# Spreading inverse row sums over the partitions: two half precision products in place of one fp32 product

## The chip, the cores and the metric

The kernel runs on one core of one Trainium2 chip. The core's engines are TensorE (PE in the profile, with its weight loads as PEld), VectorE (DVE), ScalarE (ACT), GpSimd (POOL) and SyncE (SP), which here only issues DMAs. The metric is the device time of one execution in microseconds; the time of a kernel is the median of several executions.

## What is computed

The reference is a clustered attention followed by a maxout feed-forward layer, on 4 batches, 8 heads, 768 positions and 64 features a head. Queries and keys are assigned to the nearest of 16 centroids of their head; a query sees only keys of its own cluster.

```python
q_assign = np.argmax(np.einsum('bhsd,hcd->bhsc', q_n, c_n), axis=-1)
k_assign = np.argmax(np.einsum('bhsd,hcd->bhsc', k_n, c_n), axis=-1)
mask = q_assign[:, :, :, None] == k_assign[:, :, None, :]
scores = scale * np.matmul(q, k.transpose(0, 1, 3, 2))
scores = np.where(mask, scores, -1000000000.0)
scores = scores - np.max(scores, axis=-1, keepdims=True)
attn = np.exp(scores)
attn = attn / (np.sum(attn, axis=-1, keepdims=True) + 1e-09)
x = np.matmul(attn, v)          # heads side by side: 3072 tokens of 512
h = np.maximum(np.maximum(x @ w1, x @ w2), x @ w3)
out = h @ w_out
```

What matters here is the division by the row sum. The kernel leaves the exponentials undivided, multiplies them with `v`, and multiplies the outcome with the inverse of the row sum afterwards.

## The kernel before

**Visits and steps.** The kernel works in 32 visits: for each batch, four pairs of heads times two halves of the query positions (`gi`, 384 positions each). A visit has six steps, one for each of its two heads and three tiles of 128 queries. A step (`scores`, lines 500 to 518) makes the scores of 128 queries against 768 keys with four products on PE (two at line 505, two at line 507), has DVE scale them and find the row's extreme value (510), ACT take the exponential and leave the row's sum in `rs` (513), ACT copy the outcome to half precision (515), and POOL or DVE, in turn, subtract that copy from the fp32 value (517), so that two half precision numbers stand for one of higher precision. The odd steps, the last of every visit among them, use POOL. A DMA then transposes both halves into `pt` (518).

**After a visit** come three more pieces. `av_sums` (524 to 532) takes the visit's row sums `rs`, 128 queries on the partitions and six numbers in each (three tiles, two heads). ACT adds 1e-9 (526), DVE inverts (527), and PE spreads them: for each tile and head one product with the inverse sums as weights, one column repeated 64 times, and the identity as the moving operand, puts the inverse sum of query n into column n on all 64 partitions of that head (532). It is an fp32 product; in the trace each of the six leaves two records, so a group is 12 records. `av` (534 to 546) makes the attention's output with 36 products of 64 weight columns and 384 moving columns (540). The two heads' products go to the lower and upper half of the array's columns, and so do those of line 532. `x_split` (548 to 559) copies the spread inverse sums from PSUM to SBUF on ACT (551), multiplies them with the output on DVE (553 or 555), and splits the result into two half precision numbers on POOL (557, 558).

**The rest** is preparation and the feed-forward layer. For each batch and pair of heads, `prep_units` loads queries and keys, scales and splits them, and finds the clusters (products at 444 and 448 of 64 weight columns, then DVE and POOL at 455 to 486, with DMAs that move halves between partitions). `v_prep` does likewise for `v`. The feed-forward layer's hidden products (585: 128 weight columns, 384 moving ones, twelve to a unit) and output products (619: 128 weight columns, 512 moving ones, 18 to a unit) run among the score steps of the next half batch. The very last feed-forward units stand alone at the end, from 807 us on.

**What sets the order.** Each piece of work gets a priority from the step in which it is planned (`spread`, `put`, `paced`, `plan`). A scheduler with a timing model of its own then sets the order of instructions on each engine from the priorities and from what it thinks is ready. The engines take that order as it stands. `av_sums` and `x_split` of a visit get a priority one step after the place where they are planned, and `av` five steps before it; all three are planned in the second step of the next visit. PSUM has three large buffers (`big`): one holds the output and the spread sums of a visit from the first product of `av_sums` until `x_split` has read it, and the others serve the scores.

## Time and profile before

| what | value |
|---|---|
| median of 3 runs | 858.13 us (857.68 to 858.15) |
| the profiled execution: its own time | 856.58 us |
| its span, from the first to the last instruction | 854.8 us |
| mean granted clock of TensorE | 0.928 |
| products at line 532 | 384 records, 34.6 us busy |
| ACT step at line 526, x32 | 216 ns each |
| DVE step at line 527, x32 | 182 ns each |

The profile is of one execution. A time "busy" is the time in which an engine had something running; products on PE are pipelined, so the length of a record includes the tail that runs beside the next one, and the pace of PE is read from the start of one record to the start of the next. The chain of waits is followed back from the last instruction to what released it, step by step; its shares say which engine held the end up. "Idle before" is the time that an engine stood still ahead of an instruction, with what ended it. A line such as `L532` is the kernel's line; a shape such as `128*64` is rows and columns of the array.

### The profile page before, as it was taken

What the parts mean: (1) busy time and instruction counts of PE and PEld (TensorE: products, weight loads), DVE (VectorE), ACT (ScalarE), POOL (GpSimd) and SP (SyncE); (2) the same over time, 40 slices, a digit from 0 to 9 for tenths busy, and PEclk for the clock granted to TensorE, in tenths of its full rate; (3) what the DMA queues carried; (4) which work ended last, traced back from release to release, by engine and by line L of the source; (5) the groups of instructions that cost most, each with busy time, mean ns of one, the idle gap of its engine ahead of it and who ended that gap; (6) DMA issues with size and microseconds to landing.
All of it is one profiled execution on the core that took longest, in us unless ns stands there. A gap on an engine that the chain in (4) does not pass through costs nothing.

```text
span 854.8 us, 13244 instructions
## 1 busy us (share of the span) xinstructions
PE 708.7 (83%) x4629; PEld 390.5 (46%) x4629; DVE 556.0 (65%) x1150; ACT 474.2 (55%) x837; POOL 456.1 (53%) x448
## 2 busy tenths in 40 slices
PE   2254452667989999998987899999798999999997
PEld 1122121333555455554544455555345555555563
DVE  6967858879588486368675685569768764665020
ACT  5657555776754546564663566665457465566201
POOL 1267467498676544255873654366666643454221
PEclk9995665797999999999989999999899999999999
DMA  6698795899588766678977966688978976667300
GB/s 235 127 218 178 182 222 113 185 228 201 125 178 168 154 118 127 138 140 164 188 150 155 190 133 125 146 166 159 194 158 162 154 138 136 124 112 119 86 1 37
DMA packets 329154, 128.90 MB, mean 151 GB/s; under 512 B 304384, under 2 KB 315520, under 8 KB 329088
## 3 DMA queue, kind: packets, MB, share of 16 engines
q1 hardware_dynamic: 329088, 128.06, 72.4%
q8 instruction: 36, 0.59, 0.3%
q14 instruction: 30, 0.25, 0.1%
HBM read 31.49 MB, written 6.29 MB: 44 GB/s over the span
## 4 chain that ended last, share of the span: by engine, by line
PE 52%; DVE 16%; DMA 10%; POOL 9%; issue 7%; ACT 4%; SPq 1%; POOLq 0%; DVEq 0%; ACTq 0%
PE one L585 22%; PE one L619 10%; PE big L540 8%; DMA stage<-in_qk_dram 5%; PE big L505 4%; PE big L507 4%; DVE big L510 4%; PE big L532 2%; POOL hl L517 2%; DMA stage<-in_v_dram 2%; DMA wd<-in_moe_w_dram 2%; POOL qk L417 2%; DVE hl L517 2%; DVE wf L196 2%; DMA pt<-hl 1%
## 5 line engine op out<-in xcount | busy, mean ns | idle before, releaser
L517 POOL TENSOR_TENSOR hl<-e,hl 128x768 f16<-128x768 f32 x96 | 158.6, 1652 | 162.3 <-ACT hl L515 162.3
L510 DVE TENSOR_SCALAR_CACHE_REDUCE big<-big,nsc 128x768 f32<-128x768 f32 x192 | 193.8, 1019 | 63.3 <-PE big L507 61.7
L585 PE MATMUL one<-x,w16a 128*128 128x384 f16 x1152 | 207.7, 328 | 7.0 <-DVE vpow L109 3.2
L505 PE MATMUL big<-qk 128*128 128x512 f16 (+1 forms) x384 | 105.3, 358 | 65.8 <-ACT e L513 27.5
L513 ACT ACTIVATE big<-big,nm 128x768 f32<-128x768 f32 x96 | 83.9, 874 | 127.5 <-DVE big L510 103.3
L585 PEld LDWEIGHTS <-w16a 128*128 128x128 f16 x1152 | 110.8, 98 | 87.7 <-issue 18.0
L513 ACT ACTIVATE e<-big,nm 128x768 f32<-128x768 f32 x96 | 86.7, 903 | 74.7 <-DVE big L510 65.1
L540 PE MATMUL big<-pt,v 128*64 128x384 f16 x1152 | 118.6, 344 | 1.0 <-DMA pt<-hl 0.9
L507 PE MATMUL big<-qk 96*128 96x512 f16 (+1 forms) x384 | 107.0, 359 | 13.2 <-DMA qk<-cl_t 12.1
L517 DVE TENSOR_TENSOR hl<-big,hl 128x768 f16<-128x768 f32 x96 | 91.2, 950 | 33.7 <-ACT hl L515 33.7
L585 PE MATMUL one<-x,w16b 128*128 128x384 f16 x576 | 102.8, 329 | 0.0
L505 PEld LDWEIGHTS <-qk 128*128 128x128 f16 x384 | 36.0, 102 | 123.9 <-issue 91.6
L540 PEld LDWEIGHTS <-v 128*64 128x64 f16 x1152 | 72.8, 116 | 36.8 <-issue 10.1
L515 ACT CAST hl<-e 128x768 f16<-128x768 f32 x96 | 80.1, 835 | 1.6
L515 ACT CAST hl<-big 128x768 f16<-128x768 f32 x96 | 76.7, 799 | 1.8
L585 PEld LDWEIGHTS <-w16b 128*128 128x128 f16 x576 | 55.8, 98 | 39.8 <-issue 4.4
L557 POOL TENSOR_SCALAR x<-xs 128x384 f16<-128x384 f32 x32 | 16.8, 524 | 90.7 <-DVE xs L553 78.1
L507 PEld LDWEIGHTS <-qk 96*128 96x128 f16 x384 | 40.7, 106 | 46.3 <-DMA qk<-cl_t 12.0
L381 DVE TENSOR_REDUCE q_m<-stage 128x1 f32<-128x768 f32 x32 | 30.1, 948 | 40.9 <-DMA stage<-in_qk_dram 40.9
L619 PE MATMUL one<-wo,wf_h 128*128 128x512 f16 x216 | 50.9, 379 | 0.8 <-ACT o L628 0.8
L597 DVE SCALAR_TENSOR_TENSOR wf_h<-one,wf_h 128x384 f32<-128x384 f32 x48 | 26.4, 551 | 38.6 <-PE one L585 34.6
L417 POOL TENSOR_TENSOR qk<-stage,qk 128x768 f16<-128x768 f32 x30 | 49.4, 1656 | 0.9 <-ACT qk L416 0.8
(142 smaller groups left out, 927.8 us busy)
## 6 DMA issues: line engine op xcount, KB each, us to landing
stage<-in_qk_dram SPq DMA_DIRECT2D x32, 384.0 KB, 4.2
wd<-in_moe_w_dram SPq DMA_DIRECT2D x18, 512.0 KB, 4.9
out_dram<-o SPq DMA_DIRECT2D x24, 256.0 KB, 2.8
qk<-qk SPq DMA_DIRECT2D x15, 384.0 KB, 4.7
qk<-qk SPq DMA_DIRECT2D x30, 192.0 KB, 3.8
stage<-in_v_dram SPq DMA_DIRECT2D x12, 384.0 KB, 4.9
pt<-hl SPq DMA_TRANSPOSE x192, 4.0
wd<-in_moe_w_out_dram SPq DMA_DIRECT2D x6, 512.0 KB, 4.5
```

The costliest lines, as they stand in the source:

```text
L381: nc.vector.tensor_reduce(m2[:, i : i + 1], x, axis=AX.X, op=ALU.max, apply_absolute_value=True)
L417: last["lo"] = nc.gpsimd.tensor_tensor(t[:, AQ, i], x, t[:, BQ, i], op=ALU.subtract)
L505: nc.tensor.matmul(t[:, lo:hi], aq[:, qs], ak[:, lo:hi], start=True, stop=False)
L507: last["pe"] = nc.tensor.matmul(t[:, lo:hi], bq[0:K2, qs], bk[0:K2, lo:hi], start=False, stop=True)
L510: last["nm"] = nc.vector.tensor_scalar(e, e, nsc[b, h // 2], 3.0e38, op0=ALU.mult, op1=ALU.min, accum_out=nm)
L513: last["exp"] = nc.scalar.activation(x, e, AF.Exp, bias=nm, scale=-1.0, accum_out=r)
L515: nc.scalar.copy(hl[:, 0, :], x)
L517: eng.tensor_tensor(hl[:, 1, :], x, hl[:, 0, :], op=ALU.subtract)
L540: nc.tensor.matmul(t[D * i : D * i + D, 0:NB], v[:, i, kt, a], pts[i][:, :, c * QT + kt, :], start=(n == 0), stop=(n == len(parts) - 1),)
L585: nc.tensor.matmul(t[:, 0:NB], w16[jt // JA][:, jt % JA, wa, i, ct], x16[b, gi, ct][:, xa, :], start=(n == 0), stop=(n == 3 * CT - 1),)
L597: nc.vector.scalar_tensor_tensor(m, t[:, 0:NB], 2.0**-24, ms[jt], op0=ALU.mult, op1=ALU.max)
L619: nc.tensor.matmul(t[:, 0:DM], h16[jt][:, ha, tt * P : (tt + 1) * P], wo16[0][:, jt, wa, :], start=(n == 0), stop=(n == 3 * JT - 1),)
```

## The change

The inverse sums are made into a pair of half precision numbers. After the reciprocal, ACT scales them by 2^14 and rounds to half precision (the first of the pair), and DVE scales the fp32 value by the same factor and subtracts the first (the second of the pair). In place of one fp32 product, PE makes two half precision products for each tile and head, which add up in PSUM: six become twelve. A half precision copy of the identity is the moving operand; POOL makes it once at the start. The copy from PSUM in `x_split` takes the factor out again.

```diff
+RSC = 2.0**14
...
+    identh = cpool.tile([P, P], F16, name="identh")
+    nc.gpsimd.tensor_copy(identh, ident)
...
         nc.scalar.activation(rs, rs, AF.Copy, bias=1.0e-9)
         nc.vector.reciprocal(rs, rs)
+        r16 = sb.tile([P, 2, G, 2], F16, tag="r16", name="r16", bufs=2)
+        nc.scalar.activation(r16[:, 0], rs, AF.Copy, scale=RSC)
+        nc.vector.scalar_tensor_tensor(r16[:, 1], rs, RSC, r16[:, 0], op0=ALU.mult, op1=ALU.subtract)
         for g in range(G):
             at = 512 + g * P
-            for i in range(2):
-                w = rs[:, g, i : i + 1].broadcast_to([P, D])
-                nc.tensor.matmul(t[D * i : D * i + D, at : at + P], w, ident, start=True, stop=True)
+            for a in range(2):
+                for i in range(2):
+                    w = r16[:, a, g, i : i + 1].broadcast_to([P, D])
+                    o = t[D * i : D * i + D, at : at + P]
+                    nc.tensor.matmul(o, w, identh, start=(a == 0), stop=(a == 1))
...
-        nc.scalar.copy(xs, t[:, 512 : 512 + NB])
+        nc.scalar.activation(xs, t[:, 512 : 512 + NB], AF.Copy, scale=1.0 / RSC)
```

The scheduler sets the order anew on every engine. The lines of the changed kernel stand 3 lower up to `av_sums` (505 becomes 508, 527 becomes 530) and 8 lower behind it (585 becomes 593, 619 becomes 627, `av` at 540 becomes 548); the spreading products, 532 before, are at line 540 then. Over the whole program, the order before goes between products of 64 weight columns and products of 128 on PE 204 times, the order after 270 times.

On PE, the eleventh visit's spreading products (325 us in the profile before), between hidden products of the feed-forward layer; `x` and `w16b` are that layer's operands, `v` and `pt` those of `av`. Before:

```order
L585 LDWEIGHTS w16b
L585 MATMUL one<-x_2177,w16b 128x384
L532 MATMUL big<-ident,rs 64x128 x6
L540 LDWEIGHTS v_2019
L540 MATMUL big<-pt,v_2019 64x384
L585 LDWEIGHTS w16b
L585 MATMUL one<-x_734,w16b 128x384
```

After, in the same visit, with `r` the new half precision pair and `qk` the operands of the scores:

```order
L593 MATMUL one<-x_2251,w16b 128x384
L540 LDWEIGHTS r_3052
L540 MATMUL big<-identh,r_3052 64x128
L508 LDWEIGHTS qk
L508 MATMUL big<-qk 128x512
L508 LDWEIGHTS qk
L508 MATMUL big<-qk 128x256
L510 LDWEIGHTS qk
L510 MATMUL big<-qk 128x512
L510 LDWEIGHTS qk
L510 MATMUL big<-qk 128x256
L540 LDWEIGHTS r_3052
```

The six products stood together, with the first `av` product behind them; now one of the twelve stands alone ahead of a step's score products, a second one alone ahead of the next step's, and the others follow in two pieces.

On PE, the 28th visit's (718 us before), among the output products of the feed-forward layer (`wo`, `wf_h`). Before:

```order
L619 MATMUL one<-wo_586,wf_h 128x512
L532 MATMUL big<-ident,rs 64x128
L619 LDWEIGHTS wf_h
L619 MATMUL one<-wo_586,wf_h 128x512
L532 MATMUL big<-ident,rs 64x128
L540 LDWEIGHTS v_6336
```

After:

```order
L627 MATMUL one<-wo_597,wf_h 128x512
L540 LDWEIGHTS r_7417
L540 MATMUL big<-identh,r_7417 64x128
L627 LDWEIGHTS wf_h
L627 MATMUL one<-wo_597,wf_h 128x512
L540 LDWEIGHTS r_7417
L540 MATMUL big<-identh,r_7417 64x128
```

Here three of the six stood alone between output products; now ten of the twelve do.

On DVE, the 16th visit's inverse sums (437 us before), at a change of batch; `sc_s` and `vpow` are scales of `v`, `hl` the split exponentials, `vf_h` the hidden layer. Before:

```order
L527 RECIPROCAL rs<-rs 128x6
L111 TENSOR_SCALAR sc_s<-sc_s 128x1
L517 TENSOR_TENSOR hl<-big,hl 128x768
L597 SCALAR_TENSOR_TENSOR vf_h<-one,vf_h 128x384
L510 TENSOR_SCALAR big,nm<-big,nsc 128x768
```

After, with the added step at line 533:

```order
L530 RECIPROCAL rs<-rs 128x6
L113 RECIPROCAL sc_s<-vpow 128x1
L114 TENSOR_SCALAR sc_s<-sc_s 128x1
L520 TENSOR_TENSOR hl<-big,hl 128x768
L533 SCALAR_TENSOR_TENSOR r_4356<-rs,r_4356 128x6
L605 SCALAR_TENSOR_TENSOR vf_h<-one,vf_h 128x384
```

The added step stands a subtraction behind the reciprocal, and the maximum of the hidden layer stands behind it; it waits for ACT's half of the pair, which stands behind an exponential on ACT.

## The prediction

> **What bounds the kernel now.** I read the head of the page and its chain of waits first, to see which engine sets the end, then a table by stretches, because an average over the span hides where that is so.
>
> ```profile
> span 854.8 us, 13244 instructions
> PE 708.7 (83%) x4629; PEld 390.5 (46%) x4629; DVE 556.0 (65%) x1150; ACT 474.2 (55%) x837; POOL 456.1 (53%) x448
> ...
> PE 52%; DVE 16%; DMA 10%; POOL 9%; issue 7%; ACT 4%; SPq 1%; POOLq 0%; DVEq 0%; ACTq 0%
> ```
>
> TensorE (PE) holds 52% of the chain that ended last, VectorE (DVE) 16%, ScalarE (ACT) 4%. The windows say where (length, busy time and instruction count of PE, PE's weight loads, DVE, ACT and POOL, then the granted clock and the DMA load):
>
> ```profile
> 0.00:250.00 250.00, 136.67 (x796) 68.20 (x796) 190.47 (x419) 159.77 (x268) 149.59 (x161) 0.80 0.81 183
> 250.00:400.00 150.00, 148.80 (x1001) 83.83 (x1002) 98.30 (x194) 80.03 (x144) 80.95 (x75) 1.00 0.73 147
> 400.00:500.00 100.00, 84.42 (x547) 46.89 (x545) 67.54 (x154) 52.79 (x97) 60.03 (x55) 0.93 0.80 164
> 500.00:600.00 100.00, 98.32 (x686) 55.91 (x685) 68.69 (x133) 62.29 (x112) 53.13 (x50) 1.00 0.74 144
> 600.00:660.00 60.00, 50.86 (x338) 27.29 (x338) 44.61 (x102) 33.33 (x62) 38.06 (x34) 0.94 0.86 175
> 660.00:807.00 147.00, 146.47 (x1029) 84.39 (x1026) 79.73 (x139) 81.45 (x151) 65.80 (x64) 1.00 0.70 129
> ```
>
> In three stretches (250 to 400, 500 to 600, 660 to 807) PE is busy for 393.6 of 397 us: there every tenth of a microsecond of PE counts, and nothing else does. In the other three (0 to 250, 400 to 500, 600 to 660) PE stands idle for 138 of 410 us, waiting for the preparation of the next pair or batch, and there DVE, ACT, POOL and DMA set the pace. The same query kept to line 532 says how many of the 32 groups of the changed product fall in each; a group is 12 records, two for each of six products:
>
> ```profile
> 250.00:400.00 150.00, 6.96 (x72) 4.31 (x72) 1.00 0.73 147
> 500.00:600.00 100.00, 4.14 (x48) 2.70 (x48) 1.00 0.74 144
> 660.00:807.00 147.00, 7.62 (x84) 4.97 (x84) 1.00 0.70 129
> ```
>
> So 17 groups (204 records) lie where PE is full, and 15 where it isn't.
>
> **The products themselves.** The timeline of PE in a full stretch (start, time with the pipeline's tail, what, count; the pace is read from start to start):
>
> ```profile
> 754.28 2.11 PE L585 MATMUL one<-x,w16a 128*128 128x384 f16 x12
> 756.32 0.88 PE L532 MATMUL big<-ident,rs 128*64 128x128 f32 x12
> 757.02 0.33 PE L540 MATMUL big<-pt,v 128*64 128x384 f16 x1
> 757.28 1.80 PE L585 MATMUL one<-x,w16a 128*128 128x384 f16 x10
> 758.92 0.49 PE L505 MATMUL big<-qk 128*128 128x512 f16 x2
> ```
>
> A group of six fp32 products takes 0.70 us (756.32 to 757.02). Its two heads go to the two halves of the array's columns and run side by side, so it is three slots of 0.23 us. No row shows a half precision product of 128 columns on half the array. The nearest are those of 256 columns at lines 444 and 448:
>
> ```profile
> 386.26 0.28 PE L444 MATMUL big<-qk,cw 128*64 128x256 f16 x2
> 386.37 0.28 PE L448 MATMUL big<-qk,cw 128*64 128x256 f16 x2
> ```
>
> A pair of those takes 0.11 us. If the time goes with the columns, a pair of 128 takes 0.055 us; if weight loads limit it, up to 0.11. I take 0.06, since pairs of 384 and of 256 columns both follow their columns here. The added work on PE is then six slots of 0.06, 0.36 us a group in place of 0.70.
>
> **How the order cuts the groups up.** The saving would be 17 times 0.34, or 5.8 us, if the twelve products stood together. The order shows that they don't. In the full stretches the old order has 58 slots of fp32 products (51, and 7 because of lone products); the new one has 121 slots, not 102. That is 58 x 0.23 - 121 x 0.06 = 13.3 - 7.3 = 6.0 us saved. The `av` products at line 540, 36 in a group, are cut less often: 312 slots for 320, and at 0.163 us each (10 products of line 585, also of 384 columns, take 1.64 us) that saves 1.3 us more. Against this stand the changes between half-array and full-array products, of which the new order has 146 there, where the old has 104. What one costs is read above: the lone `L540` takes 0.26 us until the next full product starts, 0.10 more than its 0.163; twelve products of line 585 take 2.04 us ahead of line 532, 0.07 more than twelve times 0.164. Lone products in the middle of line 619 show it again:
>
> ```profile
> 717.96 0.43 PE L532 MATMUL big<-ident,rs 128*64 128x128 f32 x2
> 718.33 0.39 PE L619 MATMUL one<-wo,wf_h 128*128 128x512 f16 x1
> 718.65 0.43 PE L532 MATMUL big<-ident,rs 128*64 128x128 f32 x2
> 719.01 0.39 PE L619 MATMUL one<-wo,wf_h 128*128 128x512 f16 x1
> ```
>
> I take 0.10 us a change; 42 more are +4.2 us. PE in the full stretches: -6.0 - 1.3 + 4.2 = **-3.1 us**, all of it on the path. In the other stretches PE's saving is hidden behind what it waits for: 0, at best -2.
>
> **The added ACT and DVE steps.** Their nearest rows are the steps on the same tile and a DVE step with two tensors from SBUF, like the added one:
>
> ```profile
> L526 ACT ACTIVATE rs<-rs 128x6 f32<-128x6 f32 x32 | 6.9, 216 | 0.0
> L527 DVE RECIPROCAL rs<-rs 128x6 f32<-128x6 f32 x32 | 5.8, 182 | 8.1 <-ACT rs L526 8.1
> L399 DVE SCALAR_TENSOR_TENSOR nsc<-q_p 128x1 f32<-128x1 f32 x16 | 6.6, 414 | 0.0
> L399 DVE SCALAR_TENSOR_TENSOR nsc<-q_p x16: 133/140/1557, 8.5 to 656.7; 128x1 f32<-128x1 f32 x16
> ```
>
> The ACT step costs 0.216 us. The DVE step costs 0.14 us if it runs freely and up to 1.56 if it is held; I take line 399's mean, 0.41. In the full stretches PE's queue covers both. In the others they count in part: DVE's 16% of the chain is 137 us, and if all of it lies outside the full stretches, where DVE is busy for 303 us, 0.45 of its time there is on the path; for ACT the same gives 34 of 246 us, or 0.14. For 15 groups that is 15 x 0.41 x 0.45 + 15 x 0.216 x 0.14 = 2.8 + 0.4 = **+3.2 us**. What is queued behind the new waits: on DVE, behind the step that waits for ACT's half, the next score reduction (line 510) and the maximum of the hidden layer (line 597); on ACT, behind the copy that waits for the reciprocal, the next exponential; on PE, which takes its queue in order, the next head's score products.
>
> The other edits cost nothing that shows. The scaled copy in place of the plain one (line 551) goes from 479 ns to what line 595 takes for the same shape, 490, on an engine that is 55% busy:
>
> ```profile
> L551 ACT COPY xs<-big 128x384 f32<-128x384 f32 x32 | 15.3, 479 | 44.1 <-PE big L540 44.0
> L595 ACT ACTIVATE wf_h<-one 128x384 f32<-128x384 f32 x24 | 11.8, 490 | 43.2 <-PE one L585 30.8 <-DVE wf_h L597 7.7 <-DVE cl_m L462 3.2
> ```
>
> If that cover goes, it is 32 x 0.011 = 0.35 us. POOL's one cast of the identity stands at the start, ahead of its first work. The queue of DMAs holds the same 394 transfers, some of them moved among each other. I can't price that move; two batch boundaries with the same work show what order can do there: between 400 and 500 PE idles 15.6 us, between 600 and 660 9.1, so I allow 3 us either way for it in the range and nothing in the sum.
>
> **Sum.** -3.1 + 3.2 = +0.1 us against the profiled execution's 856.58 us (span 854.8 and 1.8 around it), so 856.7. That execution lies 1.55 us under the median of 858.13, so a median of about 858.2: no change. About 0.2% (1.7 us) is what a measurement of this kernel can tell from none.
>
> **The rivals.** *Slower: the DVE step is held by POOL and the groups wait for it.* At line 399 one step of 128x1 took 1.56 us, just as long as a POOL subtraction beside it ran:
>
> ```profile
> 287.32 1.56 DVE L399 SCALAR_TENSOR_TENSOR nsc<-q_p 128x1 f32<-128x1 f32 x1
> ...
> 287.22 1.64 POOL L517 TENSOR_TENSOR hl<-e,hl 128x768 f16<-128x768 f32 x1 [5.70 <-ACT hl L515]
> ```
>
> The last head step of every visit is one whose subtraction is POOL's, and the sums are ready as it starts, so the added step may meet it nearly every time. With 1.0 us each, 15 x 1.0 x 0.45 = 6.8 in place of 2.8, and PE waits as well where it had no slack; it already did here:
>
> ```profile
> 471.88 0.88 PE L532 MATMUL big<-ident,rs 128*64 128x128 f32 x12 [0.48 <-DVE rs L527]
> ```
>
> With half a microsecond at a third of the 17 groups, +2.8: 858.2 + 4.0 + 2.8 = 865. It decides from a mean of about 0.7 us for the step. The Trainium skill, SBUF — State Buffer, Who interferes with whom, says that a DVE instruction with two SBUF inputs and a GpSimd instruction that reads SBUF exclude each other for the whole instruction; by that rule, with which line 399 agrees (1.56 us beside 1.64), the step is held whenever POOL is busy.
>
> *No gain on PE: a half precision pair costs 0.11 us, not 0.06.* Its weight load would be the limit. Then 121 slots cost 13.3 us, PE gains nothing but loses 2.9 to the changes, and the time is 858.2 + 6.0 = 864. The pairs of 256 columns can't speak against it, as 0.11 is what they take anyway. The Trainium skill, TensorE: Matmul & The Clock Gate, Back-to-back issue gap, gives about 81 ns a product for a stream of loads and products of 128 columns, 56 without the loads; with 81 a slot the sum would be 2.5 us higher, an estimate from that page. No run here shows such a pair yet.
>
> *Faster: the extra changes fall where PE waits anyway, or cost less.* PE's saving then stays near 7.3 us in the full stretches, and DVE's step runs freely (0.14 us, 15 x 0.14 x 0.45 = 0.9): 858.2 - 4.2 - 1.9 = 852. For it: the order was made with products split wherever PE had room. Against: in the full stretches PE has 3.4 us of room in all.
>
> **How the numbers follow.** My forecast, that both sides cancel within some 3 us, has 0.46, of which 0.11 falls below 856.4, 0.25 within 0.2%, 0.10 above 859.8. The held DVE step has 0.24, no gain on PE 0.05, the faster rival 0.25. So faster 0.36, same 0.25, slower 0.39. The range goes from the faster rival less the 3 us for order at a boundary (849) to the held step plus 3 (868); the forecast's own range is 855 to 861.
>
> **What would show it.** In the profile after: groups of half precision products of about 0.36 us where they stand together; 0.10 us at each change; PE's busy time down by some 3 to 5 us; the added DVE line with a mean near 0.4 us, and with lengths that end with POOL's; the idle time of PE ahead of the products still under 8 us. The forecast is wrong if the full stretches shrink by over 6 us, if they don't shrink at all, or if the stretches at the batch boundaries change by more than 4 us.

## The result and the profile after

| | before | after |
|---|---|---|
| median of 5 runs | 857.68 us (855.27 to 858.15) | 869.50 us (866.93 to 870.32) |
| ratio, 95% interval | | 1.0138 (1.0114 to 1.0162) |
| span of the profiled execution | 854.8 us | 867.7 us |
| mean granted clock of TensorE | 0.928 | 0.917 |

The changed kernel is slower by 1.4%, 11.8 us. What is read from a profile below is one execution of each kernel. The head of its page and its chain:

```profile
span 867.7 us, 13300 instructions
...
PE 713.1 (82%) x4629; PEld 391.7 (45%) x4629; DVE 570.4 (66%) x1182; ACT 475.3 (55%) x869; POOL 454.9 (52%) x449
...
PE 50%; DVE 16%; DMA 12%; issue 7%; POOL 6%; ACT 5%; SPq 3%; DVEq 0%; ACTq 0%; POOLq 0%
```

Two sums can be made from the head: PE is busy for 4.4 us more (713.1 for 708.7), and idle for 8.5 us more (867.7 - 713.1 = 154.6, where it was 146.1). The first should have been negative, the second near zero. The windows of before, read after:

```profile
0.00:250.00 250.00, 130.13 (x749) 67.22 (x750) 189.43 (x417) 156.84 (x270) 146.24 (x159) 0.79 0.77 179
250.00:400.00 150.00, 148.15 (x980) 81.73 (x979) 95.49 (x196) 80.33 (x154) 77.59 (x73) 0.98 0.69 140
400.00:500.00 100.00, 84.99 (x545) 44.87 (x544) 70.66 (x156) 51.53 (x95) 60.60 (x55) 0.90 0.84 170
500.00:600.00 100.00, 98.20 (x703) 57.09 (x702) 69.32 (x132) 60.05 (x114) 52.68 (x49) 1.00 0.77 147
600.00:660.00 60.00, 49.78 (x303) 25.88 (x302) 45.00 (x95) 29.55 (x54) 35.72 (x32) 0.89 0.85 172
660.00:807.00 147.00, 145.63 (x1017) 84.09 (x1015) 93.24 (x178) 89.52 (x173) 72.14 (x68) 1.00 0.72 129
```

Only the first stretch has much more idle time (119.9 us for 113.3), and it lies at its end, around the first change of batch. The same window in before, then after:

```profile
225.00:275.00 50.00, 46.83 (x312) 25.83 (x312) 38.80 (x88) 29.29 (x51) 37.46 (x34) 0.97 0.73 164
```

```profile
225.00:275.00 50.00, 39.17 (x242) 20.06 (x237) 34.44 (x77) 28.80 (x51) 30.90 (x28) 0.86 0.73 153
```

PE idles 3.2 us there before and 10.8 after: 7.7 of the 8.5 us. What it waits for in this window (us in total, times, longest), before:

```profile
PE big L505 <- ACT e L513: 2.5, 1, 2.5
PE big L444 <- ACT qk L416: 0.7, 1, 0.7
```

After:

```profile
PE big L508 <- ACT e L516: 4.7, 2, 3.9
PE one L109 <- DVE sc_m L107: 2.7, 1, 2.7
PE one L593 <- DVE vpow L112: 1.9, 1, 1.9
PE one L593 <- ACT vf_h L603: 1.6, 1, 1.6
```

None of these is the spreading products or the added steps: they are the exponential of the scores (L516), the scale of `v` (L107, L112) and the hidden layer (L603). A wait of this length costs twice. Three windows there (length, busy time of PE, weight loads, DVE, ACT and POOL, granted clock, DMA load), before:

```profile
240.00:245.00 5.00, 2.50 (x21) 1.47 (x20) 5.00 (x16) 3.45 (x6) 2.70 (x4) 0.87 0.86 164
245.00:250.00 5.00, 5.00 (x37) 2.60 (x34) 4.38 (x10) 2.69 (x5) 2.81 (x4) 0.79 0.83 156
250.00:255.00 5.00, 5.00 (x38) 2.93 (x38) 3.60 (x9) 2.29 (x5) 4.54 (x5) 1.00 0.61 148
```

After:

```profile
240.00:245.00 5.00, 1.11 (x8) 0.55 (x6) 5.00 (x10) 3.21 (x6) 4.49 (x5) 0.80 0.50 134
245.00:250.00 5.00, 2.28 (x8) 0.91 (x8) 5.00 (x14) 3.50 (x7) 1.91 (x2) 0.50 0.69 131
250.00:255.00 5.00, 5.00 (x22) 2.19 (x20) 4.69 (x9) 2.30 (x6) 2.62 (x3) 0.67 0.93 170
```

After the change the granted clock falls to 0.50, and nine hidden products, 1.5 us at full clock, take 3.09:

```profile
249.24 3.09 PE L593 MATMUL one<-x,w16b 128*128 128x384 f16 x9
```

That counts as busy time. The Trainium skill, TensorE: Matmul & The Clock Gate, Part 1: The HAM clock gate, says that the array falls to half rate after an idle window of some 3.4 us and comes back after as long a busy one. The trace agrees in part: its clock records have 0.50 from 243.0 to 253.2 us, three times 3.4 (before, 3.4 us at this place), but it begins 1.9 us into the wait of 3.9, when PE had not been idle for that long.

The clock settles where the 4.4 us of busy time come from. Over the whole trace PE is busy for 66.5 us at a granted clock of 0.50 before, and for 84.5 after. If half of that time is lost, as the nine products suggest, 33.3 us are lost before and 42.3 after: 9.0 more. The rest of the busy time, PE's work at full clock, goes from 675.4 to 670.9 us, 4.5 less. So the span's 12.9 us are, by this estimate, 4.5 less work, 9.0 more lost to the clock and 8.5 more idle time.

The parts of the change itself, in groups by line (busy us, mean ns, then idle before):

```profile
L540 PE MATMUL big<-identh,r 128*64 128x128 f16 x384 | 31.3, 241 | 7.6 <-DVE r L533 4.3 <-ACT e L516 2.7 <-ACT r L532 0.6
L533 DVE SCALAR_TENSOR_TENSOR r<-rs,r 128x6 f16<-128x6 f32 x32 | 20.4, 639 | 8.7 <-ACT r L532 8.4
L532 ACT ACTIVATE r<-rs 128x6 f16<-128x6 f32 x32 | 6.6, 206 | 6.4 <-DVE sc_m L106 2.7 <-DVE rs L530 2.0 <-DVE q_m L387 1.8
```

The added DVE step has a mean of 0.64 us; its shortest, median and longest in ns:

```profile
L533 DVE SCALAR_TENSOR_TENSOR r<-rs,r x32: 147/626/1631, 43.0 to 804.5; 128x6 f16<-128x6 f32 x32
```

Its six longest all end within 0.03 us of the end of a POOL instruction, so it is held as the slower rival had it. PE waited for it long only once:

```profile
194.16 0.74 PE L540 MATMUL big<-identh,r 128*64 128x128 f16 x10 [4.34 <-DVE r L533]
```

On PE, a group that stands together, and one that is cut up among output products:

```profile
223.07 0.47 PE L540 MATMUL big<-identh,r 128*64 128x128 f16 x10
223.38 0.82 PE L548 MATMUL big<-pt,v 128*64 128x384 f16 x8
...
360.04 0.24 PE L540 MATMUL big<-identh,r 128*64 128x128 f16 x1
360.21 0.39 PE L627 MATMUL one<-wo,wf_h 128*128 128x512 f16 x1
360.54 0.24 PE L540 MATMUL big<-identh,r 128*64 128x128 f16 x1
360.71 0.39 PE L627 MATMUL one<-wo,wf_h 128*128 128x512 f16 x1
```

Five pairs take 0.31 us, 0.06 each. In the second piece one lone product and one output product take 0.50 us (360.04 to 360.54); a lone slot of 0.06 and an output product's 0.215 make 0.275, so two changes cost 0.22.

Over the whole trace, the spreading products take 103 slots before and 220 after (a slot is a pair side by side, or a lone product). At 0.221 and 0.058 us a slot, as run 9 measures them below, that is 22.8 and 12.8 us, 10.0 saved. The 66 more changes cost 6.7 to 7.3 us at its 0.102 to 0.111 us each. So some 7 of the 10 us saved go to the changes, before anything is lost to the lower clock. In the last full stretch, from the 151st to the 192nd score reduction, where PE idles 1.4 us in both traces, nothing was gained: 140.0 us before, 140.6 after, with 38 changes before and 62 after.

### The profile page after: what moved, and what is told of

Same layout as the page of the kernel before. It is cut to its first block, busy times and chain, and to the rows that moved or that the text cites. A ratio compares the mean times of both kernels' runs of the same rounds, so it can differ in the third digit from the quotient of the medians.

```text
span 867.7 us, 13300 instructions
## 1 busy us (share of the span) xinstructions
PE 713.1 (82%) x4629; PEld 391.7 (45%) x4629; DVE 570.4 (66%) x1182; ACT 475.3 (55%) x869; POOL 454.9 (52%) x449
## 4 chain that ended last, share of the span: by engine, by line
PE 50%; DVE 16%; DMA 12%; issue 7%; POOL 6%; ACT 5%; SPq 3%; DVEq 0%; ACTq 0%; POOLq 0%
PE one L593 23%; PE one L627 10%; PE big L548 7%; DMA stage<-in_qk_dram 5%; DVE big L513 4%; PE big L508 4%; PE big L510 4%; DMA pt<-hl 3%; DVE hl L520 2%; SPq L521 2%; POOL hl L520 2%; PE big L540 1%; DVE wf L199 1%; DMA stage<-in_v_dram 1%; ACT hl L518 1%
## 5 line engine op out<-in xcount | busy, mean ns | idle before, releaser
L520 POOL TENSOR_TENSOR hl<-e,hl 128x768 f16<-128x768 f32 x96 | 158.6, 1653 | 138.3 <-ACT hl L518 138.1
L516 ACT ACTIVATE big<-big,nm 128x768 f32<-128x768 f32 x96 | 83.9, 874 | 117.9 <-DVE big L513 97.6
L516 ACT ACTIVATE e<-big,nm 128x768 f32<-128x768 f32 x96 | 86.6, 902 | 84.3 <-DVE big L513 69.0
L510 PE MATMUL big<-qk 96*128 96x512 f16 (+1 forms) x384 | 106.4, 357 | 13.9 <-DMA qk<-cl_t 12.8
L593 PE MATMUL one<-x,w16b 128*128 128x384 f16 x576 | 108.4, 342 | 3.0 <-DVE vpow L112 1.9
L548 PEld LDWEIGHTS <-v 128*64 128x64 f16 x1152 | 80.8, 119 | 40.0 <-issue 16.5
L508 PEld LDWEIGHTS <-qk 128*128 128x128 f16 x384 | 34.2, 101 | 107.6 <-issue 80.5
L593 PEld LDWEIGHTS <-w16b 128*128 128x128 f16 x576 | 57.6, 102 | 45.1 <-issue 11.5
L565 POOL TENSOR_SCALAR x<-xs 128x384 f16<-128x384 f32 x32 | 16.9, 530 | 108.2 <-DVE xs L561 82.5
L420 POOL TENSOR_TENSOR qk<-stage,qk 128x768 f16<-128x768 f32 x30 | 49.3, 1656 | 10.2 <-ACT qk L419 10.2
```

What stands on the lines that cost most here:

```text
L420: last["lo"] = nc.gpsimd.tensor_tensor(t[:, AQ, i], x, t[:, BQ, i], op=ALU.subtract)
L508: nc.tensor.matmul(t[:, lo:hi], aq[:, qs], ak[:, lo:hi], start=True, stop=False)
L510: last["pe"] = nc.tensor.matmul(t[:, lo:hi], bq[0:K2, qs], bk[0:K2, lo:hi], start=False, stop=True)
L516: last["exp"] = nc.scalar.activation(x, e, AF.Exp, bias=nm, scale=-1.0, accum_out=r)
L520: eng.tensor_tensor(hl[:, 1, :], x, hl[:, 0, :], op=ALU.subtract)
L548: nc.tensor.matmul(t[D * i : D * i + D, 0:NB], v[:, i, kt, a], pts[i][:, :, c * QT + kt, :], start=(n == 0), stop=(n == len(parts) - 1),)
```

## The experiments

Three theories stood at the start, and a fourth came later. **A**: the order that the scheduler makes of the changed program cuts the groups up, and each change between products of 64 and of 128 columns costs PE 0.10 us. **B**: the added ACT and DVE steps make PE wait, the DVE step above all as POOL holds it. **C**: any new order shifts the waits at the changes of batch. **D**: one DVE instruction at the first change of batch makes them. All runs but 9 in one table; "idle" is span less PE's busy time, "idle there" is that of the window from 225 to 275 us, "clock" the clock in it. These and the busy time are of one execution each, which can lie some us from the median (run 12: 863.05 for 858.65; run 17: 859.69 for 856.80). Ratios, as 95% intervals, are to the kernel before as it ran again in the same round (medians from 855.27 to 857.54 us). The expectations speak of stalls, PE's waits of over 0.3 us, which come out somewhat larger than the idle time here.

| kernel | changes | median us | ratio | PE busy | idle | idle there | clock |
|---|---|---|---|---|---|---|---|
| before | 204 | 857.68 | 1 | 708.7 | 146.1 | 3.2 | 0.97 |
| after | 270 | 869.50 | 1.0114 to 1.0162 | 713.1 | 154.6 | 10.8 | 0.86 |
| 1 after, products earlier | 188 | 859.29 | 1.0008 to 1.0040 | 696.2 | 160.3 | 12.7 | 0.90 |
| 2 before, products earlier | 208 | 854.21 | 0.9948 to 0.9986 | 708.8 | 143.9 | 3.2 | 0.97 |
| 3 after, sums in PSUM | 168 | 845.35 | 0.9812 to 0.9900 | 700.2 | 144.3 | 3.4 | 0.97 |
| 4 steps, fp32 products | 210 | 868.37 | 1.0112 to 1.0171 | 713.4 | 154.1 | 8.4 | 0.90 |
| 5 as 3, one more held step | 196 | 841.99 | 0.9800 to 0.9863 | 700.7 | 140.6 | 2.7 | 0.97 |
| 6 as 3, one more free step | 176 | 853.60 | 0.9974 to 1.0003 | 697.7 | 155.6 | 9.2 | 0.93 |
| 7 as 4, sums in PSUM | 164 | 863.19 | 1.0062 to 1.0113 | 711.1 | 151.3 | 7.3 | 0.90 |
| 8 before, sums in PSUM | 186 | 859.76 | 1.0037 to 1.0070 | 708.4 | 149.1 | 9.3 | 0.86 |
| 10 after, another order | 240 | 863.07 | 1.0058 to 1.0102 | 702.9 | 158.9 | 10.5 | 0.86 |
| 11 after, another order | 206 | 855.80 | 0.9966 to 0.9999 | 696.1 | 159.2 | 13.2 | 0.90 |
| 12 after, another order | 186 | 858.65 | 1.0008 to 1.0050 | 703.6 | 157.7 | 10.5 | 0.86 |
| 13 as 1, maximum behind | 190 | 860.26 | 1.0023 to 1.0068 | 697.1 | 158.6 | 11.9 | 0.86 |
| 14 after, maximum behind | 256 | 869.73 | 1.0122 to 1.0174 | 711.7 | 156.3 | 12.3 | 0.86 |
| 15 before, maximum ahead | 200 | 864.15 | 1.0064 to 1.0112 | 710.2 | 148.5 | 7.0 | 0.93 |
| 16 as 3, maximum behind | 158 | 842.74 | 0.9821 to 0.9868 | 689.1 | 151.9 | 4.8 | 1.00 |
| 17 products without the steps | 242 | 856.80 | 0.9975 to 1.0015 | 705.0 | 152.9 | 1.9 | 1.00 |
| 18 one product, no steps | 184 | 855.59 | 0.9964 to 0.9996 | 700.3 | 155.0 | 10.0 | 0.90 |

### First round: grouping, and the steps by themselves

**1 and 2**: one line ahead of the spreading products, in the changed kernel and in the kernel before.

```diff
+        tc.cur_priority -= 1000
         for g in range(G):
```

> The changed kernel with one more line: the spreading products get a priority one step earlier, so the scheduler sets them closer together. Work unchanged. Its order goes 188 times between products of 64 and of 128 columns (the changed kernel 270, the kernel before 204) and has 194 slots of spreading products in place of 220. Theory A (the order of the changed kernel cuts the groups up, and each change costs PE 0.10 us): PE sheds 82 x 0.10 + 26 x 0.06 = 9.8 us, most of it on the path, so 860 to 863 us. Theory B (the added ACT and DVE steps make PE wait): the steps are all still there, so 867 to 870 us. Theory C (any new order shifts the stalls at the changes of batch by several microseconds either way): no tie to the count of changes, anything from 860 to 872.

> The kernel before with the same one line: earlier priority for its six fp32 products. 208 changes for 204, 97 slots of spreading products for 103. Theory A: 0.4 us for the changes less 1.4 for the slots, so 856 to 858 us, no difference. Theory B: the same. Theory C: a new order alone may move it by 3 us or more, below 855 or above 861.

Run 1 came out at 859.29 us, a little below A's 860 to 863: PE's busy time fell by 16.9 us with 82 changes fewer. By the estimate above 6.0 of that is the clock (36.3 us lost for 42.3) and 11.0 is work, near the 9.8 that A had priced. But its idle time rose by 5.7, which A had not. Run 2 gained 0.3%, with busy time as before; its 854.21 us lies under what A and B gave, where C alone had allowed it.

**3**: the row sums go to PSUM, so that the added DVE step has one operand there.

```diff
-        nc.scalar.activation(rs, rs, AF.Copy, bias=1.0e-9)
-        nc.vector.reciprocal(rs, rs)
+        ri = t[:, 2 * 512 - 2 * G :].rearrange("p (g i) -> p g i", i=2)
+        nc.scalar.activation(ri, rs, AF.Copy, bias=1.0e-9)
+        nc.vector.reciprocal(ri, ri)
...
-        nc.scalar.activation(r16[:, 0], rs, AF.Copy, scale=RSC)
-        nc.vector.scalar_tensor_tensor(r16[:, 1], rs, RSC, r16[:, 0], op0=ALU.mult, op1=ALU.subtract)
+        nc.scalar.activation(r16[:, 0], ri, AF.Copy, scale=RSC)
+        nc.vector.scalar_tensor_tensor(r16[:, 1], ri, RSC, r16[:, 0], op0=ALU.mult, op1=ALU.subtract)
```

> The changed kernel with the inverse sums kept in PSUM, in the free columns of the visit's own buffer, between the ACT step and the added DVE step, so that this step reads one operand from PSUM and one from SBUF, not two from SBUF. If it was held by POOL, its mean falls from 0.64 us to about 0.2. The order falls out with 168 changes and 201 slots. Theory A: 102 x 0.10 + 19 x 0.06 = 11.3 us less at most, 859 to 862 us, and no better than the kernel with the earlier priority by more than 2 us. Theory B: the 4.3 us for which PE waited for the added step at 190 us go, and 15 x 0.45 x 0.45 = 3 us of DVE: 862 to 865 if the order had no part.

**4**: the added steps with the old products (the larger of the two values is taken; the low half is not used).

```diff
-        nc.vector.scalar_tensor_tensor(r16[:, 1], rs, RSC, r16[:, 0], op0=ALU.mult, op1=ALU.subtract)
+        r32 = sb.tile([P, G, 2], F32, tag="r32", name="r32", bufs=2)
+        nc.vector.scalar_tensor_tensor(r32, rs, RSC, r16[:, 0], op0=ALU.mult, op1=ALU.max)
...
-            for a in range(2):
-                for i in range(2):
-                    w = r16[:, a, g, i : i + 1].broadcast_to([P, D])
-                    o = t[D * i : D * i + D, at : at + P]
-                    nc.tensor.matmul(o, w, identh, start=(a == 0), stop=(a == 1))
+            for i in range(2):
+                w = r32[:, g, i : i + 1].broadcast_to([P, D])
+                nc.tensor.matmul(t[D * i : D * i + D, at : at + P], w, ident, start=True, stop=True)
```

> The changed kernel with its added ACT and DVE steps, the latter writing the larger of the scaled inverse sum and its half precision copy as fp32, and the six fp32 products of the kernel before made from that. It has the whole chain of waits and none of the half precision products; the low half is not used. 210 changes and 119 slots of 0.23 us, where the kernel before has 204 and 103. Theory A: 857.7 + 0.6 + 16 x 0.23 x 0.6 = 860 to 862 us. Theory B: the steps make the difference, so 866 to 870 us.

Run 3 fell to 845.35 us, below both kernels and below what either theory gave; its added step ran freely, in 157 ns:

```profile
L534 DVE SCALAR_TENSOR_TENSOR r<-big,r 128x6 f16<-128x6 f32 x32 | 5.0, 157 | 6.8 <-ACT r L533 6.8
```

Run 4 stood at 868.37, as B had it. Together they looked like B. The next round was made to break that.

### Second round: is it the held step?

**5 and 6**: run 3 with one more DVE step ahead of the second half, with two operands from SBUF (5) or one from PSUM (6).

```diff
+        nc.vector.scalar_tensor_tensor(r16[:, 1], rs, 1.0, rs, op0=ALU.mult, op1=ALU.subtract)
```

```diff
+        nc.vector.scalar_tensor_tensor(r16[:, 1], ri, 1.0, rs, op0=ALU.mult, op1=ALU.subtract)
```

> The kernel with the inverse sums in PSUM (845.35 us, span 844.5) with one more DVE step ahead of the second half of the pair: it takes the row sums from SBUF as both of its operands and its result is overwritten. So a step that POOL can hold stands again in the chain, and the products wait for it. 196 changes for 168, 208 slots for 201. Theory B (what costs is that such a step is held): its mean is 0.5 to 0.7 us and PE's stalls come back, 8 to 10 us, with 28 x 0.10 for the changes: 853 to 858 us. Theory A (changes alone): 845.4 + 28 x 0.10 + 7 x 0.06 = 848 us.

> As the kernel with the held extra step, but the extra step takes one operand from PSUM and one from SBUF. 176 changes, 203 slots. Theory B: the step runs in 0.16 us, 846 to 848 us (845.4 + 8 x 0.10 + 15 x 0.16 x 0.45 = 847). If not the hold but the mere number of steps in the chain costs, it comes out where the kernel with the held extra step does, 853 to 858.

**7 and 8**: run 4 and the kernel before, with the sums in PSUM as in run 3 (in run 8 the reciprocal reads them there and writes `rs`).

> The added ACT and DVE steps with the fp32 products, as in the kernel that took 868.4 us, but with the inverse sums in PSUM, so that the added DVE step has one operand from PSUM. 164 changes for its 210, 103 slots of 0.23 us for 119; the low half is not used. Theory B: of its 10.7 us over the kernel before, all but the steps' own time goes, 15 x (0.16 x 0.45 + 0.17 x 0.14) = 1.4 us: 856 to 860 us. Theory A: 46 x 0.10 + 16 x 0.23 = 8.3 us at most, about 5 on the path, 863 us.

> The kernel before with one edit: the row sums with 1e-9 added go to PSUM and DVE's reciprocal reads them there. No step of two SBUF operands is in it, with or without the edit. 186 changes for 204, 106 slots for 103. Theory B: no difference from before but for the changes, 18 x 0.10 less 3 x 0.23 = 1.1 us at most: 855 to 858 us. If the place of the sums alone or the new order explains the 845 us, it falls to 850 or less.

B's times for runs 5 and 6 both missed, in opposite directions. The held step takes 399 ns on the mean in run 5 (median 165, where the step in the changed kernel had 626, so it is held less often), the free one 155 in run 6:

```profile
L534 DVE SCALAR_TENSOR_TENSOR r<-rs 128x6 f16<-128x6 f32 x32 | 12.8, 399 | 2.6 <-ACT e L516 2.6
```

```profile
L534 DVE SCALAR_TENSOR_TENSOR r<-big,rs 128x6 f16<-128x6 f32 x32 | 5.0, 155 | 2.5 <-ACT r L533 2.4
```

Yet run 5, where PE waits 6.4 us in six pieces for the step behind the held one, is with run 16 the fastest of all, 841.99, and run 6 takes 853.60. Run 7 came out at A's 863 us (863.19), not at B's 856 to 860. Run 8, at 859.76, has no added step and no half precision product, and its idle time between 225 and 275 us is 9.3 us, nearly that of the changed kernel. So B can't be the whole cause, and the place of the sums alone does not give run 3's time. Run 8 waits there for:

```profile
PE big L505 <- ACT e L513: 5.1, 1, 5.1
PE big L505 <- DVE q_m L384: 4.1, 2, 3.4
```

### Third round: prices, and other orders of the same program

**9** measures prices alone; it leaves the whole computation out.

> Leaves the whole computation out: PE runs products of the kernel's shapes back to back, alone, in groups and in alternation, and DVE runs the added step beside POOL subtractions. From the traces so far: a pair of half precision products of 128 columns 0.06 us, an fp32 pair 0.23, a change between 64 and 128 weight columns 0.10. If the price of a change is real, twelve of them in a unit cost about 1.2 us where two cost 0.2; if it is the wait for something else in the kernel, alternation costs nothing here. The added step with two operands from SBUF is held for most of a POOL subtraction (1.6 us), with one from PSUM it takes 0.16.

Windows of that run, each over 120 products of one kind or 120 of each of two: half precision pairs alone, fp32 pairs alone (240 records), products of 128 x 384 alone; then half precision and 128 x 384 products in groups of 12, two and two in turn, one and one in turn (a few records fall on the other side of a window's edge):

```profile
34.15:37.62 3.47, 3.47 (x118) 3.23 (x118) 0.00 (x0) 0.00 (x0) 1.00 0.02 5
57.23:70.48 13.25, 13.25 (x240) 13.02 (x240) 0.00 (x0) 0.00 (x0) 1.00 0.01 2
70.48:90.08 19.60, 19.60 (x126) 11.72 (x122) 0.00 (x0) 0.00 (x0) 1.00 0.00 1
119.56:144.67 25.11, 25.11 (x242) 14.56 (x240) 0.00 (x0) 0.00 (x0) 1.00 0.01 1
144.67:181.07 36.40, 36.40 (x242) 13.28 (x240) 0.00 (x0) 0.00 (x0) 1.00 0.00 1
181.07:234.03 52.96, 52.96 (x242) 24.01 (x240) 0.00 (x0) 0.00 (x0) 1.00 0.00 0
```

A half precision pair takes 3.47 / 60 = 0.058 us, an fp32 pair 13.25 / 60 = 0.221. In groups, 25.11 - 3.47 - 19.60 = 2.04 us for 20 changes, 0.102 each. Two and two, 36.40 - 23.07 = 13.33 for 120, 0.111 each. One and one, where each lone product fills a slot, 52.96 - 120 x 0.058 - 19.60 = 26.4 for 240, 0.110 each. So the same 240 products take 25 us or 53, by their order alone.

The held step, beside POOL subtractions (DVE first, then POOL; L105 has both operands in SBUF, L108 one in PSUM):

```profile
7.07 1.50 DVE L105 SCALAR_TENSOR_TENSOR d<-rs,r 128x6 f16<-128x6 f32 x1
8.48 0.15 DVE L108 SCALAR_TENSOR_TENSOR d<-pr,r 128x6 f16<-128x6 f32 x1
```

```profile
6.89 1.65 POOL L106 TENSOR_TENSOR hl<-e,hl 128x768 f16<-128x768 f32 x1
8.62 1.65 POOL L103 TENSOR_TENSOR hl<-e,hl 128x768 f16<-128x768 f32 x1
```

The first ends at 8.57 as POOL's does at 8.54. Of its six executions three were held (1.04, 1.50 and 1.50 us) and three took 0.15 to 0.17. With an operand in PSUM it takes 0.15 to 0.17 us whatever POOL does (18 of them, mean 161 ns). That the held ones end with POOL's instruction agrees with the Trainium skill, SBUF — State Buffer, Who interferes with whom. But not every step beside POOL is held: one of the free three began at 5.59 us, within a POOL subtraction that the trace has from 5.17 to 6.81.

**10 to 12** are the changed kernel with the line of run 1 at 5, -500 and 6000 in place of 1000: the same instructions in other orders.

> The changed kernel in another order: the spreading products' priority is earlier by five thousandths of a step. Nothing else differs. 240 changes and 213 slots, where the changed kernel has 270 and 220. PE's time without stalls over 0.3 us is 695.4 us there and 692.4 before; here I expect 686 to 688. Theory A (stalls as before, 151 us): 850 to 852 us. Theory B (the steps bring 8 to 10 us of stalls): 859. Theory C (stalls come from the order, 149 to 168 us whatever the steps): 686 + 149 to 168 + 13 = 848 to 869, and the three new orders of this program differ by 6 us or more in their stalls.

> As the one before, with the products' priority half a step later: 206 changes, 201 slots. PE's time without stalls: 681 to 682 us. Theory A: 846 us. Theory B: 855. Theory C: 843 to 864.

> As the one before, with the products' priority six steps earlier: 186 changes, 192 slots. PE's time without stalls: 678 to 680 us. Theory A: 843 us. Theory B: 852. Theory C: 841 to 861.

With the changed kernel and run 1 that makes five orders of one program: 855.80, 858.65, 859.29, 863.07 and 869.50 us. The one that the change got is the slowest, with the most changes and the most busy time. A's times for runs 10 to 12 (850 to 852, 846 and 843 us) all missed; of B's (859, 855 and 852) one came true. C as I had put it, that the idle time of these three differs by 6 us or more, fell: they differ by 1.5, all five by 5.7 (154.6 to 160.3).

What differs is PE's busy time, and most of that goes with the changes. By the estimate above, work at full clock is 670.9 us with 270 changes, 665.1 with 240, 661.3 with 206, 661.2 with 186 and 659.9 with 188; on top of that, 34.8 to 42.5 us are lost to the clock. Less work need not mean less time: run 11 has 14.2 us less of it than the kernel before (675.4), 13.1 more of idle time, 1.6 more lost to the clock, and takes as long.

### Fourth round: the 7.7 us at the first change of batch

In the trace of after, the maximum over a load of queries and keys waits 3.0 us for its DMA at the head of DVE's queue, at 236 us, with score reductions behind it; in the kernel before two more score reductions stand ahead of it. **13, 14 and 16** move it back behind the 47th score reduction, in run 1, the changed kernel and run 3 (`nms` lists the score reductions); **15** moves it ahead of the 46th in the kernel before, with an edit that is not shown.

```diff
+    nms = []
+    HOLD = {(1, 2, 1): 46}
...
         for i, x in enumerate(xin[b, pr]):
-            nc.vector.tensor_reduce(m2[:, i : i + 1], x, axis=AX.X, op=ALU.max, apply_absolute_value=True)
+            with ExitStack() as st:
+                if (b, pr, i) in HOLD:
+                    st.enter_context(tc.issue_after(nms[HOLD[b, pr, i]].ins))
+                nc.vector.tensor_reduce(m2[:, i : i + 1], x, axis=AX.X, op=ALU.max, apply_absolute_value=True)
...
+        nms.append(last["nm"])
```

> The changed kernel with the earlier priority of the products (859.29 us, stalls 168.3), and one DVE instruction moved: the maximum over the second load of queries and keys of batch 1, pair 2, stands behind the 47th score reduction, where the kernel before has it, and not behind the 45th. Else the orders agree (PE 20 lines of some 9,000, DVE 10). Theory D (that maximum waits for a DMA with two score reductions queued behind it, and that makes the stalls between 225 and 275 us): stalls there fall from 13.6 to 4 to 7 us, the whole to 851 to 854 us. If the stalls there come from the added steps (theory B), it stays at 859.

> The changed kernel itself (869.5 us) with the same DVE instruction moved behind the 47th score reduction. The order of PE shifts more here: 256 changes for 270. Theory D: stalls between 225 and 275 us fall from 11.8 to 4 to 6 us; with 14 x 0.10 for the changes, 861 to 864 us. Theory B: 867 to 869.

> The converse: the kernel before (856 to 858 us), with that maximum ahead of the 46th and 47th score reductions, as the changed kernel has it. No added step, no half precision product; 200 changes for 204. Theory D: stalls between 225 and 275 us rise from 3.5 to 9 to 12, and it takes 861 to 865 us. Theory B: no difference, 856 to 858.

> The kernel with the inverse sums in PSUM (845.35 us), with the maximum behind the 47th score reduction in place of the 46th. Its stalls between 225 and 275 us are 3.8 us already; 158 changes for 168. Theory D: 842 to 846 us, nothing much left to gain there.

D fell in its main test: run 13 differs from run 1 by little more than that instruction, and nothing came of it (860.26 for 859.29); nor did run 14 gain, 869.73 for D's 861 to 864. The wait only moved; PE's waits in the window, run 13:

```profile
PE big L513 <- ACT e L522: 6.1, 1, 6.1
PE big L547 <- ACT r L538: 2.0, 1, 2.0
PE one L600 <- ACT vf_h L610: 1.9, 1, 1.9
```

The converse held in part: run 15 is slower by 0.9% (its profiled execution, of 858.7 us span, is its fastest, and shows 3.8 us more of idle time there). But its edit does more than move one maximum: it ties the 46th score reduction behind that maximum and plans two pieces of the preparation two and three steps earlier, and 177 of PE's 4629 products stand elsewhere for it, all of them between 232 and 277 us in before. So an order that differs at this place alone is enough to cost 0.9%. That the maximum does it is not shown, and undoing that one place is not enough to cure it.

**17** leaves out the added steps and keeps the twelve products, with the first half of the pair in the place of the second; **18** keeps only six. The edit of 17:

```diff
-        nc.vector.reciprocal(rs, rs)
...
-        nc.scalar.activation(r16[:, 0], rs, AF.Copy, scale=RSC)
-        nc.vector.scalar_tensor_tensor(r16[:, 1], rs, RSC, r16[:, 0], op0=ALU.mult, op1=ALU.subtract)
+        with nc.allow_low_precision(reason="half"):
+            nc.vector.reciprocal(r16[:, 0], rs)
...
-                    w = r16[:, a, g, i : i + 1].broadcast_to([P, D])
+                    w = r16[:, 0, g, i : i + 1].broadcast_to([P, D])
...
-        nc.scalar.activation(xs, t[:, 512 : 512 + NB], AF.Copy, scale=1.0 / RSC)
+        nc.scalar.activation(xs, t[:, 512 : 512 + NB], AF.Copy, scale=0.5)
```

> The twelve half precision products without the added steps: DVE's reciprocal writes half precision itself, and both halves of a pair are that number (so the low half is left out and the copy takes out a factor of 2). No added ACT step, no added DVE step, the chain as long as before. 242 changes, 209 slots. PE busy about 703 us, as in the order of the changed program with 240 changes. If the added steps bring about the idle time at 225 to 275 us (by their wait or by what the scheduler makes of it): PE idle there 3 to 5 us as before, 146 to 149 in all, a span of 850 and a median of 851 to 853 us. If any new order can do it: idle 7 to 13 there, 154 to 160 in all, 858 to 864.

> As the kernel with the products alone, but only one half precision product for each tile and head (six, not twelve; the low half is left out). 184 changes, 96 slots. PE busy 690 to 697 us: 96 x 0.06 in place of 103 x 0.23 is 18 us less than before, of which the lower clock after waits takes some. With PE idle 146 to 149 us, a median of 838 to 848; with 154 to 160, 846 to 858.

Run 17 has 1.9 us idle there, run 18 has 10.0, and neither has an added step. So the idle time at this place comes and goes with the order: it is there in every order of the changed program (after, 1 and 10 to 14), but also in 8 and 18 without the steps, and not in 3 and 5 with them. Run 17 also takes as long as before, 856.80 us; its profiled execution, 2.9 us above that median, has 3.7 us less of busy time and 6.8 more of idle time. So little idle time there does not by itself make a kernel faster: it stood elsewhere.

## Why the prediction was wrong, point by point

**The prices were right.** A half precision pair 0.06 (0.058 measured alone), an fp32 pair 0.23 (0.221), a change 0.10 (0.102 to 0.111). The rival that gave the pair 0.11 is out, and the Trainium skill's figure that was weighed there, TensorE: Matmul & The Clock Gate, Back-to-back issue gap, 81 ns a product, does not describe two products side by side: a pair takes 58.

**PE's sum of -3.1 us** was about right for PE's work: over the whole trace, slots and changes give -10.0 + 7.0 = -3.0, and the work at full clock fell by 4.5 us. It did not show in the busy time, which rose by 4.4, as 9.0 us more were lost to the granted clock of 0.50. A saving was counted at full clock, and nothing in the sum stood for what a new wait does to it. Nor was it all on the path: the last full stretch did not shrink.

**The added steps, +3.2 us.** The ACT step took 206 ns (216 put in). The DVE step was held more often than line 399's: 0.64 us, not 0.41, so 15 x 0.23 x 0.45 = 1.6 us more by the same working. That term was mis-sized, by far less than the 11.8 us.

**The step that failed** is the one on the order, there of the DMA transfers among each other: "I can't price that move [...] I allow 3 us either way for it in the range and nothing in the sum." The new waits of the engines on each other had no other term. The 3 us came from two batch boundaries of one order. What was put at nothing there came out, over the whole trace, at 8.5 us more of idle time, 7.7 of them at the first change of batch, and 9.0 us more lost to the clock. The forecast of no change had assumed that stretches which wait go on waiting as long as they did; the prediction's own test, that the boundaries must not change by more than 4 us, is where it broke.

That the order alone is worth the 11.8 us is shown by runs 1 and 10 to 12: the same instructions in four other orders took 6 to 14 us less, in run 11 no longer than the kernel before. They did so by PE's busy time. None of them lost the idle time at the first change of batch, so that part of the cost stays without a cure and without a shown reason.

**The slower rival had the sign and not the cause.** A held DVE step, 865 us. The step is held, as it said, and PE waited for it once for 4.34 us, but from 175 to 200 us, where that was, PE idled 11.2 us (12.9 before): that wait stood in for others. In run 11 the step is held nearly as long (618 ns on the mean), and the kernel takes 855.80 us, so the hold is not enough for the 11.8. Run 5, with a step in the chain that is held less often, is with run 16 the fastest kernel here, and runs 8 and 18 have the idle time without any such step. What a hold as frequent as that in the changed kernel costs by itself was not measured: the seven kernels with the half precision products and the sums in SBUF (after, 1 and 10 to 14) took 855.80 to 869.73 us, the four with the sums in PSUM 841.99 to 853.60, so some part of it may lie there in every order.

**What stays open.** Which property of the order makes the idle time between 225 and 275 us. The held step and the added steps are neither needed for it (runs 8 and 18) nor enough (runs 3 and 5), and moving the one maximum back does not end it. Nor is it shown why the sums in PSUM gave 842 to 845 us in three of four kernels with the half precision products: the fourth, with a free step more, took 853.60. About half of their lead stands before the first change of batch: the 25th score reduction starts at 147.2 us in before, at 141.6, 139.6 and 140.5 in runs 3, 5 and 16, and at 150.6 in run 6.

## What to carry to other kernels

Where a scheduler sets the order, a change has two effects, its own and that of the new order, and the second can be the larger: here 13.7 us between the medians of five orders of one program, while the products without the steps, in the one order that was tried, took as long as before (run 17). A profile's busy time holds what a lower clock adds: set apart the time at each granted clock before a saving is looked for in it. Price the change from rows, then try the same program in a few other orders before judging it; one line of priority was enough, and took back 6 to 14 us. Products that use half of the array's columns should stand together, since a change to full ones costs nearly two such pairs.

## What the runs showed of the hardware

- Going between products of 64 and of 128 weight columns costs 0.10 to 0.11 us each way, for half precision products alone as in the kernel. The Trainium skill, TensorEngine Tiling (Array Packing), Key Properties, says that a change of tiling mode drains the engine; the cost here is two pairs of 128 columns.
- Around waits of 3.9 and 2.7 us on PE the granted clock stood at 0.50 for 10.2 us, and nine products took twice their time. Over the trace, PE was busy at 0.50 for 66.5 us before and 84.5 after.
- A DVE step of 6 elements with both operands in SBUF took up to 1.63 us beside POOL, ending with POOL's instruction, and 0.16 with one in PSUM.
